# Attention, two dense blocks and SOLU on one core: x by token tile, a first chunk kept in SBUF, and stores moved to GpSimd

## The chip, the cores and the metric

The kernel runs on 1 core of one Trainium2 chip (8 cores; the others are idle). The metric is the device time of one execution in microseconds, as the median of several runs.

## The reference

`x` is (8, 8, 512, 64): 8 batches, 8 heads, 512 tokens, 64 wide. `state` is (8, 8, 32, 64). The weights come as 64-bit floats.

```python
scores = scale * x @ state.T                 # per batch and head
a = softmax(scores)                          # over the 32 states
xread = a @ state
a2 = softmax(scale * state @ x.T)            # over the 512 tokens
sread = a2 @ x
x = concat([xread, sread], tokens)           # 8 * (512 + 32) rows of 512
x = relu(x @ moe_w_in) ** 2 @ moe_w_out      # 512 -> 2048 -> 512
h = x @ moe2_w_in                            # 512 -> 1024
solu = h * softmax(h)
out = (layernorm(solu) * g_ln) @ moe2_w_out  # 1024 -> 512
```

## The kernel before

Products are made of float32 parts: each operand is split into a high and a low part, and `triple` adds three products (high by high, high by low, low by high) in one PSUM bank. The 64-bit weights are fetched as integer words, and `convert_parts` makes the two parts with six VectorE and two ScalarE operations, spread over the calls of `advance`.

Instead of `xread @ moe_w_in` the kernel forms state times weights first: `sw_part(u, j)` multiplies a block of states by unit u of w1_in (u = 4c + hp: chunk c of 512 columns, head pair hp). j = 0 serves batches 0 and 1, j = 1 batches 2 and 3. The products are evicted by ScalarE to `ev_sw` (L317), stored to DRAM in `sw_d` (L319, L321), and loaded back in another layout by `load_sw(b, c)` (L387), which gives one staging tile for each batch and chunk; `split_sw` makes the two parts. `hidden` (L134 to L136, tile `ps_h`) multiplies the softmax of a batch by them, and `project` (tile `acc`) adds the result of one f (128 of the 2048 hidden columns) times w1_out.

`attention(b)` is a list of 15 pieces. For batches 0 and 1: `trans_x` transposes one head pair of x (L125), splits it with an extra product (`split_bank`), `scores_t` makes scores, `rows_a` and `rows_b` the softmax of tokens (the last operation of `rows_b` is L491), `trans_a` transposes it for `hidden`, `cols_a`, `cols_b` and `cols_t` make the softmax of states, and `sread` multiplies it with x (L525). All these share two PSUM banks. `state_step(a_st, t)` transposes the states of batches 2t and 2t + 1 (tile `ps_st`) and splits them; `a_st` is filled from DRAM by `load_state_rows` (L273).

The opening fetches w1_in units 0 to 3 (`fetch_pair`, L647), x of batch 0 on ScalarE's queue (L424), the state rows; then runs the pieces of `attention(0)` between conversions of units 0 to 3 and `sw_part(u, 0)`; then `sw_part(u, 1)` and the rest of `attention(0)`. The main loop goes over 144 steps s of (batch, f), 16 f to a batch; batches 0 and 1 share the first 32 steps and alternate by chunks of four. `attention(1)` is put into steps 0 to 3 and the attention of a later batch into the 16 steps before it is needed. The table `when` gives the step at which each unit of w1_out ("o") and w1_in ("i") begins its conversion; fetches go out two steps earlier, and `sw_part` runs two steps later. Partial sums of a batch that is left go to `x2p_d` (L630). A converted w1_in part is also stored in `w1i_d` (L233) for later use.

Each engine takes its instructions in a fixed order that the build chose, mostly that of the program. All DMAs are issued by SyncE's queue (SP), except x of batch 0, and a DMA that waits for its data holds everything behind it on its queue. Staging tiles (`stg`), eviction tiles (`ev`) and the converted w1_in tiles have 4, 2 and 4 buffers.

Of the kernel before, what the change touches and what calls it, by code (L numbers as in the profile page):

```python
# [20 lines left out]
def memory_attention_relu2_solu(  # L21
# [15 lines left out]
    nc = tc.nc  # L37
# [48 lines left out]
    xsp = pool("xsp", 4, sa, side="right")  # L86
# [9 lines left out]
    mhalf = const.tile([P, 1], F32, name="mhalf")  # L96
    rebias = const.tile([P, 1], F32, name="rebias")
# [128 lines left out]
    def convert_w1in(u, st):  # L226

        c, k = divmod(u, NM)

        t = u_tile("w1in")  # L230

        def done():
            nc.sync.dma_start(out=w1i_d[k][:, :, c * FC : (c + 1) * FC], in_=t.bitcast(F32))  # L233
            w1u[u] = t

        flying.append(convert_parts(st, t[:, 0, :], t[:, 1, :], done))
# [28 lines left out]
    def load_state():  # L265
        a = wp.tile([P, B, NQ, 2, D], F32, tag="w", name="a_st")
        nc.vector.memset(a[:, :2], 0.0)
        nc.gpsimd.memset(a[:, 2:], 0.0)
        return a

    def load_state_rows(a, b0, b1):
        for h in range(4):
            nc.sync.dma_start(  # L273
                out=a[h * NS : (h + 1) * NS, b0:b1, :, h % 2, :],
                in_=state[b0:b1].rearrange("b (q h) n d -> h n b q d", h=4)[h],
            )

    def state_step(a, t):

        if t == 0:  # L280
            bdw[0] = wp.tile([P, 2, NQ, 4, 2 * NS, 2], F32R, tag="w", name="bdw")
            nc.vector.memset(bdw[0].bitcast(F32), 0.0)
# [18 lines left out]
    def sw_part(u, j):  # L301
# [3 lines left out]
        single = c == 0 and j < 2  # L305
        if j % 2 == 0 or single:
            sw_ev[0] = evp.tile([P, 2, 512], F32, tag="ev", name="ev_sw")
# [9 lines left out]
        nc.scalar.activation(out=ev[:, j % 2, :], in_=ps, func=AF.Copy)  # L317
        if single:
            nc.sync.dma_start(out=sw_d[hp][:, j, c * FC : (c + 1) * FC], in_=ev[:, j % 2, :])  # L319
        elif j % 2 == 1:  # L320
            nc.sync.dma_start(out=sw_d[hp][:, j - 1 : j + 1, c * FC : (c + 1) * FC], in_=ev)  # L321
# [96 lines left out]
    def load_x(b, hps=range(NHP), eng=None):  # L418
        if b == 1:
            both = wp.tile([P, NHP, NT, 2, D], F32, tag="w", name="xs_w")  # L420
        for hp in hps:
            t = both[:, hp] if b == 1 else xsp.tile([P, NT, 2, D], F32, tag="xs", name="xs")
            for i in range(2):
                (eng or nc.sync).dma_start(out=t[:, :, i], in_=x[b, 2 * hp + i].rearrange("(p t) d -> p t d", t=NT))  # L424
            xs_t.setdefault(b, []).append(t)

    def attention(b):
# [3 lines left out]
        def trans_x(hp):  # L431
            ps = bank("ps_x")
            transposes(ps, [xs_t[b][hp][:, t].rearrange("p h d -> p (h d)") for t in range(NT)])
# [83 lines left out]
        def sread(half):  # L517
# [3 lines left out]
            for hp in (2 * half, 2 * half + 1):  # L521
                for t in range(NT):
                    for i in range(2):
# [3 lines left out]
                            lhsT=xs_t[b][hp][:, t, i, :],  # L527
# [82 lines left out]
    def project(blk, f, n, gh, gl, m):  # L610
# [7 lines left out]
        if last:  # L618
# [9 lines left out]
            if m % 2 == 1:  # L628
                to = x2p_d[blk] if f + 1 < NF else x2_d[blk]
                nc.sync.dma_start(out=to[:, m - 1 : m + 1, :], in_=x2_ev[0][:, :, :n])  # L630
# [22 lines left out]
    nc.gpsimd.memset(rebias, -float(896 << 23))  # L653
    make_identity(nc, ident)
    fetch_pair(0, 0)
    load_x(0, eng=nc.scalar)
    a_st = load_state()
    load_state_rows(a_st, 0, 2)
    nc.scalar.activation(out=negi, in_=ident, func=AF.Copy, scale=-1.0)
    nc.gpsimd.memset(mhalf, -0.5)  # L660
# [6 lines left out]
    load_state_rows(a_st, 2, B)  # L667
# [12 lines left out]
    load_sw(0, 0)  # L680
# [4 lines left out]
    begin("o", 0)  # L685
    state_step(a_st, 1)
    for i in range(4):
        fetch_pair(NM + 2 * (i // 2), i % 2)
# [118 lines left out]
    when |= {("i", u): w for u, w in zip(range(AHEAD, NU), (1, 2, 3, 4, 7, 8, 9, 10, 13, 15, 16, 18))}  # L807
# [16 lines left out]
    for s, (b, f) in enumerate(items):  # L824
# [43 lines left out]
        if s == 2 * FPC - 1:  # L868
            load_sw(*chunks[2])
# [11 lines left out]
        if s // FPC + 1 < len(chunks) and chunks[s // FPC + 1][0] < B:  # L881
# [3 lines left out]
            elif s % FPC == 1:  # L885
                load_sw(*nxt)
# [101 lines left out]
```

## Time and profile before

| what | value |
|---|---|
| runs | 1136.05, 1141.4, 1140.76 us; median 1140.76 |
| profiled execution | 1139.05 us, its span 1137.3 us |
| TensorE (PE) busy | 1104.1 us, 97% |
| VectorE (DVE) busy | 706.0 us, 62% |
| ScalarE (ACT) busy | 512.7 us, 45% |
| GpSimd (POOL) busy | 43.1 us, 4% |
| mean granted clock of PE | 0.994 |

Busy shares are means over the whole span; the first 84 us differ from the rest. A granted clock of 1.00 is the upper of the two levels of PE (2.4 GHz). Lines such as L134 are those of the kernel before. "A <-B" at the end of a row of the timeline tells how long the engine had been idle and who released it.

### The profile page before, as it was taken

To read this page: it belongs to the slowest core of one execution; us is meant where nothing else is said; L and a number is where in the kernel's file an instruction comes from. 1 tells how busy PE (TensorE), PEld (TensorE's weight loads), DVE (VectorE), ACT (ScalarE), POOL (GpSimd) and SP (SyncE) were. 2 spreads that over 40 slices of the span, in tenths; PEclk is the share of its full clock that TensorE was granted. 3 is DMA by queue.
4 is the path that set the end of the run, shared out by engine and by line. 5 is a ranking of instruction groups with operands and counts; after the bars stand their busy time and mean duration, and the time that the engine had idled before them with its cause. 6 is when DMAs were issued, how large, how long until landed. Compare 5 with 4: busy or idle time off the path is not lost.

```text
span 1137.3 us, 15226 instructions
## 1 busy us (share of the span) xinstructions
PE 1104.1 (97%) x5692; PEld 911.9 (80%) x5692; DVE 706.0 (62%) x1358; ACT 512.7 (45%) x902; POOL 43.1 (4%) x59
## 2 busy tenths in 40 slices
PE   5779999999999999999999999999999999999997
PEld 3557888878888888888888889988888888888886
DVE  6389987479578488685675545664545545455442
ACT  4778987555355354342343213352433434334332
POOL 0000000001000010010000000000000000000000
PEclk9889999999999999999999999999999999999999
DMA  8688986478776652412211126420101101000010
GB/s 221 205 223 279 322 269 167 138 207 228 200 214 183 183 175 93 139 56 72 77 38 56 38 75 238 165 80 19 56 28 57 65 19 39 27 19 28 19 28 29
DMA packets 93962, 135.75 MB, mean 119 GB/s; under 512 B 45376, under 2 KB 45888, under 8 KB 93888
## 3 DMA queue, kind: packets, MB, share of 16 engines
q1 hardware_dynamic: 89664, 133.73, 37.9%
q10 hardware_dynamic: 4224, 1.05, 0.5%
q8 instruction: 45, 0.74, 0.3%
q14 instruction: 29, 0.24, 0.1%
HBM read 84.41 MB, written 50.33 MB: 118 GB/s over the span
## 4 chain that ended last, share of the span: by engine, by line
PE 88%; ACT 4%; DVE 4%; DMA 2%; issue 1%; ACTq 0%; SPq 0%; POOLq 0%; POOL 0%
PE h L738 16%; PE acc L134 10%; PE acc L136 10%; PE acc L135 10%; PE ps_h L134 6%; PE ps_o L789 5%; PE ps_h L135 5%; PE ps_h L136 5%; PE ps_o L787 5%; PE ps_o L788 5%; PE ps_t L777 2%; PE ps_sr L525 1%; PE ps_x L125 1%; PE ps_a L125 1%; DMA st<-in_moe_w_in_dram 1%
## 5 line engine op out<-in xcount | busy, mean ns | idle before, releaser
L134 PE MATMUL acc<-gh,w1out 128*128 128x512 f32 (+1 forms) x576 | 218.5, 381 | 0.5 <-ACT w1out L215 0.5
L135 PE MATMUL acc<-gl,w1out 128*128 128x512 f32 (+1 forms) x576 | 217.7, 378 | 0.1
L136 PE MATMUL acc<-gh,w1out 128*128 128x512 f32 (+1 forms) x576 | 217.3, 378 | 0.0
L738 PE MATMUL h<-w,x2h 128*128 128x512 f32 x544 | 148.6, 395 | 0.0
L584 ACT ACTIVATE r<-ps_h 128x512 f32<-128x512 f32 (+1 forms) x144 | 82.5, 573 | 132.0 <-PE ps_h L136 130.7
L586 DVE TENSOR_TENSOR r<-r,ps_h 128x512 f32<-128x512 f32 (+1 forms) x112 | 72.5, 647 | 88.6 <-ACT r L584 88.2
L134 PEld LDWEIGHTS acc<-gh,w1out 128*128 128x128 f32 x576 | 109.0, 189 | 21.9 <-ACT w1out L215 0.9
L136 PEld LDWEIGHTS acc<-gh,w1out 128*128 128x128 f32 x576 | 108.4, 188 | 20.7
L135 PEld LDWEIGHTS acc<-gl,w1out 128*128 128x128 f32 x576 | 108.4, 188 | 20.6 <-DVE gl L600 0.3
L738 PEld LDWEIGHTS h<-w,x2h 128*128 128x128 f32 x544 | 99.7, 188 | 18.8
L600 DVE TENSOR_TENSOR gl<-r,gh 128x512 fp32r<-128x512 f32 (+1 forms) x144 | 97.5, 677 | 17.7 <-ACT r L593 14.6
L134 PE MATMUL ps_h<-ah,sw 128*128 128x512 f32 x256 | 107.2, 420 | 0.9 <-ACT sw L113 0.9
L787 PE MATMUL ps_o<-w,lh 128*128 128x512 f32 x272 | 106.0, 390 | 1.0 <-ACT lh L113 1.0
L789 PE MATMUL ps_o<-w,ll 128*128 128x512 f32 x272 | 106.2, 390 | 0.6 <-DVE ll L114 0.6
L788 PE MATMUL ps_o<-w,lh 128*128 128x512 f32 x272 | 105.8, 389 | 0.0
L756 ACT ACTIVATE e<-h,nm 128x1024 f32<-128x1024 f32 x34 | 38.0, 1117 | 143.7 <-DVE nm L753 143.7
L136 PE MATMUL ps_h<-ah,sw 128*128 128x512 f32 x256 | 100.8, 396 | 0.0
L135 PE MATMUL ps_h<-al,sw 128*128 128x512 f32 x256 | 100.1, 393 | 0.0
L752 DVE TENSOR_REDUCE nm<-h 128x1 f32<-128x1024 f32 x34 | 41.6, 1225 | 83.2 <-PE h L738 83.2
L738 PE MATMUL h<-w,x2l 128*128 128x512 f32 x272 | 83.8, 389 | 0.0
L764 ACT ACTIVATE j<-e,mu 128x1024 f32<-128x1024 f32 x34 | 39.1, 1151 | 54.3 <-DVE mu L761 50.4
L114 DVE TENSOR_TENSOR sw<-stg,sw 128x512 fp32r<-128x512 f32 x64 | 44.4, 698 | 28.5 <-ACT sw L113 28.2
(162 smaller groups left out, 1734.4 us busy)
## 6 DMA issues: line engine op xcount, KB each, us to landing
stg<-sw_d SPq DMA_DIRECT2D x128, 128.0 KB, 3.3
sw_d<-ev_sw SPq DMA_DIRECT2D x28, 512.0 KB, 3.8
st<-in_moe_w_out_dram SPq DMA_DIRECT2D x24, 512.0 KB, 5.4
w1i_d<-w1in SPq DMA_DIRECT2D x16, 512.0 KB, 4.1
st<-in_moe_w_in_dram SPq DMA_DIRECT2D x16, 512.0 KB, 5.8
w1in<-w1i_d SPq DMA_DIRECT2D x32, 256.0 KB, 4.6
x_d<-ev_x SPq DMA_DIRECT2D x16, 512.0 KB, 2.7
w1in<-w1i_d SPq DMA_DIRECT2D x16, 512.0 KB, 5.3
```

The source lines that it names most:

```text
L114: nc.vector.tensor_tensor(out=lo, in0=src, in1=hi.bitcast(F32), op=ALU.subtract)
L134: nc.tensor.matmul(out=ps, lhsT=lh, rhs=rh, start=first and i == 0, stop=False)
L135: nc.tensor.matmul(out=ps, lhsT=lh, rhs=rl, start=False, stop=False)
L136: nc.tensor.matmul(out=ps, lhsT=ll, rhs=rh, start=False, stop=last and i == n - 1)
L584: nc.scalar.activation(out=r, in_=ps, func=AF.Relu)
L586: nc.vector.tensor_tensor(out=r, in0=r, in1=ps, op=ALU.mult)
L600: nc.vector.tensor_tensor(out=gl, in0=r, in1=gh.bitcast(F32), op=ALU.subtract)
L738: nc.tensor.matmul(out=ps[:, a * 512 : (a + 1) * 512], lhsT=lt[:, k, t * P : (t + 1) * P], rhs=w2[k][:, i, a * 512 : (a + 1) * 512], start ...
L752: nc.vector.tensor_reduce(out=nm, in_=ps, axis=AX.X, op=ALU.max)
L787: nc.tensor.matmul(out=ps, lhsT=a, rhs=wt[:, 0, o : o + 512], start=(k == 0), stop=False)
L788: nc.tensor.matmul(out=ps, lhsT=a, rhs=wt[:, 1, o : o + 512], start=False, stop=False)
L789: nc.tensor.matmul(out=ps, lhsT=bb, rhs=wt[:, 0, o : o + 512], start=False, stop=(k == NK - 1))
```

## The change

x of a batch is loaded in four DMAs, one for each token tile t with all 8 heads, into one tile instead of four tiles of a head pair; batch 0's loads go from ScalarE's queue to SP's, and the first state rows from SP's to ScalarE's. The pool of x tiles has one buffer. A one-column activation runs ahead of everything on ScalarE. The memset of `bdw` moves from VectorE to GpSimd.

The products of chunk 0 for j = 0 go from `ev_sw` straight to the staging tiles of batches 0 and 1 by SBUF-to-SBUF copies; `load_sw(0, 0)` and `load_sw(1, 0)` are gone. In chunk 0 two head pairs share one `ev` tile.

The fetches of w1_in units 4 to 7 stand ahead of the splitting of the first chunk; the state rows of batches 2 to 7 are loaded later, ahead of `state_step(a_st, 1)`. Units 4 to 7 begin one step earlier, and `load_sw` of the third chunk stands one step earlier. The stores of w1_in parts, of the other sw products and of partial sums are issued by GpSimd.

```diff
-    xsp = pool("xsp", 4, sa, side="right")
+    xsp = pool("xsp", 1, sa, side="right")
...
+    warm = const.tile([P, 1], F32, name="warm")
...
         def done():
-            nc.sync.dma_start(out=w1i_d[k][:, :, c * FC : (c + 1) * FC], in_=t.bitcast(F32))
+            nc.gpsimd.dma_start(out=w1i_d[k][:, :, c * FC : (c + 1) * FC], in_=t.bitcast(F32))
...
-        nc.gpsimd.memset(a[:, 2:], 0.0)
...
-            bdw[0] = wp.tile([P, 2, NQ, 4, 2 * NS, 2], F32R, tag="w", name="bdw")
-            nc.vector.memset(bdw[0].bitcast(F32), 0.0)
...
-        single = c == 0 and j < 2
-        if j % 2 == 0 or single:
+
+        single = c == 0
+        at = i if single else j
+        if at == 0:
             sw_ev[0] = evp.tile([P, 2, 512], F32, tag="ev", name="ev_sw")
...
-        nc.scalar.activation(out=ev[:, j % 2, :], in_=ps, func=AF.Copy)
-        if single:
-            nc.sync.dma_start(out=sw_d[hp][:, j, c * FC : (c + 1) * FC], in_=ev[:, j % 2, :])
-        elif j % 2 == 1:
-            nc.sync.dma_start(out=sw_d[hp][:, j - 1 : j + 1, c * FC : (c + 1) * FC], in_=ev)
+        nc.scalar.activation(out=ev[:, at, :], in_=ps, func=AF.Copy)
+        if single and j == 0:
+
+            for b in range(2):
+                if hp == 0:
+                    loading[b, 0] = stgp.tile([P, 2, 512], F32, tag="stg", name="stg")
+                nc.sync.dma_start(
+                    out=loading[b, 0][i * 2 * NS : (i + 1) * 2 * NS, hp // 2, :], in_=ev[b::2, at, :]
+                )
+        elif single:
+            nc.gpsimd.dma_start(out=sw_d[hp][:, j, c * FC : (c + 1) * FC], in_=ev[:, at, :])
+        elif j == 1:
+            nc.gpsimd.dma_start(out=sw_d[hp][:, j - 1 : j + 1, c * FC : (c + 1) * FC], in_=ev)
...
+    def load_x(b):
+        pl, tag = (wp, "w") if b == 1 else (xsp, "xs")
+        xs_t[b] = pl.tile([P, NT, H, D], F32, tag=tag, name="xs")
+        for t in range(NT):
+            nc.sync.dma_start(out=xs_t[b][:, t], in_=x[b].rearrange("h (p t) d -> t p h d", t=NT)[t])
...
-                nc.sync.dma_start(out=to[:, m - 1 : m + 1, :], in_=x2_ev[0][:, :, :n])
+                (nc.gpsimd if f + 1 < NF else nc.sync).dma_start(out=to[:, m - 1 : m + 1, :], in_=x2_ev[0][:, :, :n])
...
     nc.gpsimd.memset(rebias, -float(896 << 23))
+    nc.scalar.activation(out=warm, in_=rebias, func=AF.Copy)
     make_identity(nc, ident)
     fetch_pair(0, 0)
-    load_x(0, eng=nc.scalar)
+    load_x(0)
     a_st = load_state()
-    load_state_rows(a_st, 0, 2)
+    load_state_rows(a_st, 0, 2, nc.scalar)
+    bdw[0] = wp.tile([P, 2, NQ, 4, 2 * NS, 2], F32R, tag="w", name="bdw")
+    nc.gpsimd.memset(bdw[0].bitcast(F32), 0.0)
+    nc.gpsimd.memset(a_st[:, 2:], 0.0)
+    nc.gpsimd.memset(mhalf, -0.5)
     nc.scalar.activation(out=negi, in_=ident, func=AF.Copy, scale=-1.0)
-    nc.gpsimd.memset(mhalf, -0.5)
...
     state_step(a_st, 0)
-    load_state_rows(a_st, 2, B)
     load_x(1)
...
     sw_part(NM - 1, 0)
-    load_sw(0, 0)
+    for i in range(4):
+        fetch_pair(NM + 2 * (i // 2), i % 2)
     while len(att) > 5:
...
     begin("o", 0)
+    load_state_rows(a_st, 2, B, nc.sync)
     state_step(a_st, 1)
-    for i in range(4):
-        fetch_pair(NM + 2 * (i // 2), i % 2)
...
-    when |= {("i", u): w for u, w in zip(range(AHEAD, NU), (1, 2, 3, 4, 7, 8, 9, 10, 13, 15, 16, 18))}
+    when |= {("i", u): w for u, w in zip(range(AHEAD, NU), (0, 1, 2, 3, 7, 8, 9, 10, 13, 15, 16, 18))}
...
-        if s == 2 * FPC - 1:
+        if s == 2 * FPC - 2:
             load_sw(*chunks[2])
...
             elif s % FPC == 1:
-                load_sw(*nxt)
+                if nxt not in loading:
+                    load_sw(*nxt)
```

## Rows read from the trace of the kernel before

**Rows 1.** The page's 40 equal slices: PE's busy share, in tenths.

```profile
PE   5779999999999999999999999999999999999997
```

**Rows 2.** Stages of the span: length, each engine's busy time, granted clock, DMA.

```profile
core 0: us, PE busy (x) PEld busy (x) DVE busy (x) ACT busy (x) POOL busy (x), PEclk, DMA share, GB/s
0.00:13.00 13.00, 1.95 (x9) 1.58 (x9) 6.00 (x11) 3.77 (x7) 2.10 (x9) 1.00 0.87 226
...
28.10:33.80 5.70, 0.93 (x7) 0.72 (x8) 5.70 (x17) 3.36 (x7) 0.00 (x0) 0.89 0.80 300
33.80:38.80 5.00, 4.94 (x17) 3.20 (x17) 0.54 (x2) 3.48 (x7) 0.00 (x0) 0.50 0.00 0
38.80:48.10 9.30, 8.08 (x94) 6.35 (x94) 1.27 (x3) 5.28 (x11) 0.00 (x0) 0.97 0.55 174
48.10:65.30 17.20, 16.65 (x79) 12.20 (x77) 10.24 (x19) 15.38 (x29) 0.00 (x0) 1.00 0.89 272
65.30:72.40 7.10, 2.30 (x9) 1.63 (x10) 6.39 (x18) 4.24 (x8) 0.00 (x0) 0.84 0.96 192
72.40:84.00 11.60, 10.66 (x96) 8.69 (x95) 11.23 (x28) 8.07 (x16) 0.00 (x0) 0.81 0.77 248
84.00:180.00 96.00, 95.00 (x423) 76.55 (x423) 89.43 (x175) 82.31 (x150) 0.00 (x0) 1.00 0.85 278
```

**Rows 3.** Timeline of the first 13 us: start, duration, engine, line, operation.

```profile
0.74 7.83 ACTq L424 DMA_DIRECT2D xs<-in_x_dram  x8
1.42 3.70 SPq L273 DMA_DIRECT2D a_st<-in_state_dram  x4
8.14 1.09 PE L287 MATMUL ps_st<-ident,a_st 128*128 128x128 f32 x4 [8.14 <-DMA a_st<-in_state_dram]
8.65 1.28 ACT L203 ACT_TABLE_LOAD   x1 [8.65 <-DVE bdw L282]
9.02 1.06 PE L125 MATMUL ps_x<-ident,xs 128*128 128x128 f32 x4
12.85 0.58 ACT L118 ACTIVATE xh<-ps_x 128x512 fp32r<-128x512 f32 x1
```

**Rows 4.** Timeline of SP's queue from 39 to 49 us.

```profile
39.28 1.20 SPq L319 DMA_DIRECT2D sw_d<-ev_sw  x2
...
44.75 2.00 SPq L647 DMA_DIRECT2D st64w<-in_moe_w_in_dram  x4
...
48.49 0.64 SPq L157 DMA_DIRECT2D st<-in_moe_w_out_dram  x1
```

**Rows 5.** Timeline of PE and ACT between 26 and 48 us.

```profile
26.01 0.39 PE L136 MATMUL ps_sw<-w1in,bdw 128*128 128x512 f32 x1
37.23 1.12 PE L287 MATMUL ps_st<-ident,a_st 128*128 128x128 f32 x4
38.67 0.59 ACT L317 ACTIVATE ev_sw<-ps_sw 128x512 f32<-128x512 f32 x1
47.02 0.62 ACT L113 ACTIVATE sw<-stg 128x512 fp32r<-128x512 f32 x1
```

**Rows 6.** Timeline of DVE from 57 to 70 us, three of its operations.

```profile
57.31 0.43 DVE L202 TENSOR_SCALAR cz<-st 128x512 uint32<-128x512 uint32 x1
...
60.22 0.68 DVE L208 SCALAR_TENSOR_TENSOR cu<-st,cu 128x512 f32<-128x512 uint32 x1
...
69.64 0.68 DVE L491 TENSOR_TENSOR e<-e,sm 128x512 f32<-128x512 f32 x1
```

**Rows 7.** DMA issues of the opening: count, KB each, median us to landing.

```profile
a_st<-in_state_dram SPq DMA_DIRECT2D x4, 96.0 KB, 7.8
```

**Rows 8.** Stores of converted w1_in on SP: issue in ns, minimum, median, maximum.

```profile
L233 SPq DMA_DIRECT2D w1i_d<-w1in x16: 512/554/1155, 24.3 to 159.1; - x16
```

**Rows 9.** A later window's loads of x, their time to landing, and first transposes.

```profile
387.86 2.83 SPq L424 DMA_DIRECT2D xs<-in_x_dram  x4
396.49 0.60 PE L125 MATMUL ps_x<-ident,xs 128*128 128x128 f32 x4
DMA to landing us min/median/max: 2.5/3.3/6.5
```

More of the change, by code (lines that the diff above doesn't have):

```diff
@@ L267, in load_state, with load_state_rows @@
         nc.vector.memset(a[:, :2], 0.0)
-        nc.gpsimd.memset(a[:, 2:], 0.0)
         return a
-    def load_state_rows(a, b0, b1):
+    def load_state_rows(a, b0, b1, eng):
         for h in range(4):
-            nc.sync.dma_start(
+            eng.dma_start(
                 out=a[h * NS : (h + 1) * NS, b0:b1, :, h % 2, :],
@@ L278, in state_step @@
     def state_step(a, t):
-        if t == 0:
-            bdw[0] = wp.tile([P, 2, NQ, 4, 2 * NS, 2], F32R, tag="w", name="bdw")
-            nc.vector.memset(bdw[0].bitcast(F32), 0.0)
         ps = bank("ps_st")
@@ L416, in memory_attention_relu2_solu @@
     a1_t = {}
[L418 to L425, printed above, removed]
+    def load_x(b):
[3 more added lines that the diff above has]
+            nc.sync.dma_start(out=xs_t[b][:, t], in_=x[b].rearrange("h (p t) d -> t p h d", t=NT)[t])
     def attention(b):
@@ L432, in trans_x @@
             ps = bank("ps_x")
-            transposes(ps, [xs_t[b][hp][:, t].rearrange("p h d -> p (h d)") for t in range(NT)])
+            transposes(ps, [xs_t[b][:, t, 2 * hp : 2 * hp + 2].rearrange("p h d -> p (h d)") for t in range(NT)])
             xh = xtp.tile([P, S], F32R, tag="xh", name="xh")
@@ L526, in sread @@
                             out=ps[i * D : (i + 1) * D, hp * NS : (hp + 1) * NS],
-                            lhsT=xs_t[b][hp][:, t, i, :],
+                            lhsT=xs_t[b][:, t, h, :],
                             rhs=v["e2", t // 2][:, t % 2, h * NS : (h + 1) * NS],
```

## The prediction, made before the change was run

> **What bounds the kernel now.** I began with the page's 40 slices. TensorE (PE) is short of full in the first three slices and the last one [rows 1], so a change to the opening can only win what the opening loses. Then I cut the opening into stages and read busy time and granted clock of each [rows 2]; PE's busy time there subtracts from the length to give its idle time.
>
> - 0 to 13 us: PE idles 11.05 us. The timeline of the start [rows 3] says why: the state rows arrive at 8.14 us, the first x transposes run at 9.02, but ScalarE (ACT) has spent its queue on eight x loads until 8.57, loads its table from 8.65 to 9.93, and takes up `xh`, which is waiting since about 10.1, only at 12.85.
> - 28.1 to 33.8: 4.77 us idle: the softmax of `attention(0)`, alone.
> - 33.8 to 38.8: full, but at granted clock 0.50, which is the lower of the two levels (1.2 GHz); it had fallen after the idle stretch. The same work at the upper level would be about 2.5 us shorter.
> - 38.8 to 48.1: 1.22 us idle. The first `hidden` could not start before its chunk had gone to DRAM and back: evicted at 38.67, stores issued from 39.28, and only from 47.02 split by ACT for the products [rows 4, 5].
> - 48.1 to 65.3: 0.55 us idle; ACT is busy 15.38 of 17.20.
> - 65.3 to 72.4: 4.80 us idle, and here VectorE (DVE) is busy 6.39 of 7.10. PE stands at `trans_a` of `attention(1)`, whose last DVE operation runs at 69.64 [rows 6]. The clock falls again: 0.84 over 7.10 us and 0.81 over the next 11.60 us make 2.3 + 4.4 = 6.7 us at the lower level; PE had work in about 6.2 of them, a loss of 3.1.
> - 72.4 to 84: 0.94 us idle. 84 to 180: 1.00 us idle in 96, DVE busy 89.43.
>
> From 84 us on PE is full. So the change can win part of what lies before, and it can lose anywhere, if it slows DVE or delays a buffer.
>
> **The change, part by part.** The sum goes against the profiled execution, 1139.05 us, which is 1.7 below the median of the three runs.
>
> *Start.* ACT loses the eight x issues and gets four issues of state rows; a one-column activation asks for the table early; the 2048-element memset leaves DVE for GpSimd (Pool). ACT's part of the delay goes: after the transposes of x, `xh` can be taken at once. What now sets the start is whether data arrive. The state rows wait on ACT for the table load: at most 1.28 us later than 8.14 [rows 3], at best no later. x needs all of its 1 MB before the first transpose (the tile is cut by token, where before a head pair was enough), but the DMA engines moved 226 GB/s over 0 to 13 us [rows 2], 1.6 MB by about 9 after the first bytes at about 2. I take PE's start at 9.0; two sets of transposes took 1.94 us (8.14 to 10.08), so `xh` starts at 10.9 in place of 12.85: **-2.0** (bounds -2.8 at 8.14, -1.5 at 9.4). Pool has nothing else then, and its memsets are needed only at about 9.
>
> *State rows of batches 2 to 7*, moved on SP from ahead of x of batch 1 to behind the j = 0 copies and four weight loads. They feed `state_step(1)`, which ran at 37.23 [rows 5], with PE's in-order queue behind it: the j = 1 products, `cols_t`, `sread`, `attention(1)`. With -2.0 it could run at 35.2. The last j = 0 product ended at 26.4 [rows 5], so now at about 24.4; its copies go out by 26, four weight loads take 2.00 us [rows 4], so the first rows go out at about 28 and the last by 30; their landing took 7.8 [rows 7]. That gives 36 to 38, or 34 where the engines are free sooner: **+1.0** (0 to +3.0). This is the one place where a move adds a wait.
>
> *First chunk from SBUF to SBUF.* Four stores of 256 KB to DRAM and eight reloads become eight copies of 128 KB, and no load waits for a store any more. Two `ev` halves per tile also remove the wait of the third eviction for the first store. The chunk is ready before `trans_a` ends. PE was short by only 1.22 us there, as it had other work: **-0.8** (0 to -1.2). Chunk (1, 0) came from DRAM too; it no longer does, but the wait it caused ACT lay beside DVE's, so nothing.
>
> *Next weights at another place.* The loads of w1_in units 4 to 7 move ahead of SP's waits: from 44.75 to about 26; the load of w1_out 1, at 48.49, follows them up [rows 4]. DVE was busy 1.27 of 9.30 and 0.54 of 5.00 us before 48.1 [rows 2], and then had to convert while `attention(1)` waited: one tile is three masks of 0.43 and three operations of 0.68 us, 3.3 in all. Between the mask at 57.31 and the operation at 69.64 [rows 6] lie twelve conversion operations, one whole tile and half of two more; they are some 6.5 us, and as each starts a little before the last one ends, about 5.3 of DVE's time. With data and free DVE time earlier, and unit 4 begun a step earlier by the table of due steps, these go ahead of the chain. The chain to `trans_a` then shortens by up to 5.3, the idle 4.80 us shrink, and the clock has less reason to fall (3.1). All of it would be -7.9; I take the chain's 5.3 and a little of the clock: **-5.5** (0 to -7.9). After 84 us all must still be fed by DVE; it can, as the same operations only moved earlier.
>
> *38 stores on Pool* (16 of w1_in parts, 16 of sw products, 6 of partial sums). On SP such a store takes 0.51 to 1.16 us of issue, 0.55 in the median [rows 8], and SP stood behind stores that waited for their data, which held the loads in [rows 4]. Freed, this gain is already counted above. No Pool DMA occurs before, so its price is unknown: below, nothing (Pool is idle); above, that each holds a DVE operation for an issue, 0.55 us as on SP up to 0.98, ACT's mean for the x loads [rows 3]. I take nothing, since the consumers are steps away, and keep the rest as a rival. The Trainium skill, DMA: Bandwidth & Descriptors, "Issuing engines are not separate DMA queues", says that another issuing engine saves only the sequencer's issue time; by it the move would give about 38 x 0.55 us of SP time and nothing to PE. Here the queue's order is what counts, not the issue.
>
> *x tiles of later batches.* One tile in place of four, so all loads wait for the last `sread`. In the window shown they then start at 387.86. If four loads of twice the size issue in the 2.83 us of four before, they land 3.3 later, at 394.0, and PE wants them at 396.49 [rows 9]: 2.5 us to spare. If the issue takes twice as long, they are 0.3 late; if the landing takes the longest seen, 6.5, more. I take the first, 0.
>
> Sum: -2.0 + 1.0 - 0.8 - 5.5 = -7.3, **1131.8 us**.
>
> **Rivals.**
>
> *A: the moved waits eat it.* The chain from `attention(0)` to `attention(1)` is one line: if the state rows come at the late bound (+3.0), the start's 2.0 and the first chunk's 0.8 are spent, and the conversions give only about 2: 1137. For it: PE is in order and the rows are last in SP's queue. Against: the DMA engines moved nothing from 33.8 to 38.8 [rows 2], so there is room for them to come.
>
> *B: Pool's stores hold DVE (slower).* Some 28 of the 38 fall after 84 us, where DVE has 96 - 89.43 = 6.57 us left [rows 2]. At 0.98 each it is 27.4 - 6.6 = 20.8 lost, 1152; at 0.55, 8.8, 1140. From 0.50 a store, (7.3 + 6.6) / 28, it undoes the gain, from 0.70 the kernel is slower by over 0.5%. For it: DVE's masks of 512 elements take 0.43 beside 0.68 for two-input operations of the same size [rows 6], so they run in some faster mode of their own, which another engine's work may cost them. Against: no row here shows Pool and DVE in each other's way, and an idle Pool takes 38 issues easily. The Trainium skill, SBUF — State Buffer, "Who interferes with whom", says that a DVE operation in a two-port mode and a GpSimd operation lock each other out of a shared port pair for a whole instruction, and that stores from GpSimd wait for descriptors so long. By that the stores land later, and masks may wait; no run here shows its size.
>
> *C: the x tile is late.* If the larger loads issue in twice 2.83 us and land after 6.5, they come at 400.0, 3.5 us late [rows 9]; in five windows (batches 3 to 7) that is 17.5, 1149. It makes the kernel slower than before from 1.5 us a window. Against: 3.3 is the median, and the spare of 2.5.
>
> *D: PE's gaps close and the clock stays up.* If the early chunk also fills the 4.77 us at 28.1 to 33.8 and both low stretches (2.5, 3.1) shrink: another 8 of these 10.4 us, 1124. Against: in that gap nothing but `attention(0)` can be ready.
>
> **How the numbers follow.** Forecast 0.50, A 0.26, B 0.13, C 0.04, D 0.07. A measurement here can tell about 0.5%, 5.7 us. The forecast and D are faster by more: 0.57; A is within: 0.26; B and C slower: 0.17. The likeliest alone spans 1126 to 1135. For 8 in 10 the range reaches over A and the lower part of B, and down to D: 1122 to 1143.
>
> **What would show it.** Right: `xh` at about 11 us in place of 12.85; the first `ps_h` well before 48; w1_out 1 converted on DVE before 57; the idle stretch before `trans_a` of `attention(1)` below 3 us, the end of the opening some 8 us earlier, and the later windows as long as before. Wrong: PE waiting on `a_st` at about 35 to 39; DVE operations after 84 us longer or with idle time before them that Pool ends; PE waiting for x at the start of a window; or an order of conversions on DVE that has not moved.

## The result, and the profile after

The changed kernel takes 1147.86 us in the median (1147.20 to 1149.77, 5 runs), beside 1140.76 us (1136.05 to 1141.40, 5 runs) of the kernel before on the same chip: ratio 1.0082, 95% interval [1.0067, 1.0096]. It is slower by 0.8%, against a forecast of 1131.8 us, and outside the range of 1122 to 1143. The two medians alone differ by less, 7.1 us or 0.6%, since the kernel before scattered here; in the later runs its medians lie between 1137.64 and 1138.33, which 1147.86 exceeds by 0.8 to 0.9%. The profiled execution took 1149.77 us with a span of 1147.9 us, 10.6 more than before.

The page's 40 slices of PE, which answer to [rows 1], look no worse than before:

```profile
PE   5888989999999999999999999999999999999997
```

The stages do [rows 2]; the columns are the same.

```profile
0.00:13.00 13.00, 4.59 (x13) 2.87 (x13) 5.71 (x12) 5.49 (x11) 4.65 (x11) 1.00 0.97 237
28.10:33.80 5.70, 1.28 (x5) 0.94 (x6) 5.70 (x17) 4.85 (x10) 0.00 (x0) 0.79 0.97 350
33.80:38.80 5.00, 4.74 (x14) 3.54 (x14) 1.53 (x4) 2.78 (x5) 0.00 (x0) 0.56 0.84 166
38.80:48.10 9.30, 7.93 (x36) 5.82 (x36) 4.91 (x11) 8.37 (x16) 0.74 (x1) 1.00 0.50 191
48.10:65.30 17.20, 16.98 (x137) 13.15 (x136) 16.74 (x36) 14.23 (x28) 3.95 (x6) 1.00 0.89 275
65.30:72.40 7.10, 4.26 (x22) 3.08 (x21) 6.45 (x17) 4.35 (x8) 0.10 (x1) 1.00 0.18 74
72.40:84.00 11.60, 11.12 (x74) 8.45 (x75) 8.94 (x22) 9.34 (x19) 1.45 (x2) 0.71 0.33 98
84.00:180.00 96.00, 87.91 (x410) 69.70 (x407) 76.02 (x149) 72.47 (x133) 15.83 (x23) 0.98 0.75 256
```

Up to 84 us PE is busy 4.35 us more than before. From 84 to 180 it idles 8.09 in place of 1.00, and DVE is busy only 76.02 in place of 89.43, so DVE has time to spare: 9.5 us of its work had been done before 84 us already (62.40 us busy in place of 52.91), and in 84 to 180 it waits, mostly for ACT. The later windows keep their length (the first `sread` product of batch 7 stands 6.3 us later than before, that of batch 2 stood 6.1 later), and some 4 us more are lost behind 820 us.

The start answers to [rows 3] (start, duration, engine, line, operation): the table is loaded at once, and `xh` is taken at 10.73 in place of 12.85.

```profile
0.74 1.28 ACT L658 ACT_TABLE_LOAD   x1 [0.74 <-PEq L980]
8.37 1.09 PE L284 MATMUL ps_st<-ident,a_st 128*128 128x128 f32 x4 [8.37 <-DMA a_st<-in_state_dram]
10.73 0.59 ACT L119 ACTIVATE xh<-ps_x 128x512 fp32r<-128x512 f32 x1
```

Between 20 and 33 us SP's queue holds the copies of the first chunk, the next weights, which go out 18.5 us earlier than in [rows 4], and then the state rows:

```profile
20.00 6.23 SPq L322 DMA_DIRECT2D stg<-ev_sw  x7
26.27 2.10 SPq L651 DMA_DIRECT2D st64w<-in_moe_w_in_dram  x4
28.47 4.12 SPq L273 DMA_DIRECT2D a_st<-in_state_dram  x4
```

PE in the same stretch answers to [rows 5]. The first `hidden` product runs at 35.55 (before: 48.10), and all four hidden tiles of it stand ahead of `state_step(1)`, which runs at 42.51 (before: 37.23) without waiting for its rows. `attention(1)` begins at 52.33 (before: 44.57).

```profile
35.55 0.63 PE L135 MATMUL ps_h<-ah,sw 128*128 128x512 f32 x1
...
42.51 0.60 PE L284 MATMUL ps_st<-ident,a_st 128*128 128x128 f32 x4
...
52.33 0.66 PE L126 MATMUL ps_x<-ident,xs 128*128 128x128 f32 x4
```

DVE [rows 6]: the last two operations before `trans_a` of `attention(1)` run from 72.06 to 73.34; before, the last one ended at 70.32, 3.0 us earlier. Their chain on DVE, from the first maximum on, is shorter than before, 6.0 us (67.31 to 73.34) in place of 8.9 (61.42 to 70.32, the first line below is of the kernel before), but it begins 5.9 us later, when PE delivers `ps_r`. Masks and two-input operations take as long as before (0.41 to 0.43, and 0.68).

```profile
61.42 0.68 DVE L476 TENSOR_REDUCE mx<-ps_r 128x16 f32<-128x512 f32 x1
```

```profile
57.20 0.41 DVE L203 TENSOR_SCALAR cz<-st 128x512 uint32<-128x512 uint32 x1
...
58.20 0.68 DVE L209 SCALAR_TENSOR_TENSOR cu<-st,cu 128x512 f32<-128x512 uint32 x1
...
67.31 1.29 DVE L480 TENSOR_REDUCE mx<-ps_r 128x16 f32<-128x512 f32 x2 [0.65 <-PE ps_r L470]
...
72.06 1.28 DVE L495 TENSOR_TENSOR e<-e,sm 128x512 f32<-128x512 f32 x2
```

The late state rows land in 7.8 us, as before [rows 7]. The issue of a w1_in store now takes 0.69 us on Pool in the median, 0.55 on SP before [rows 8]. The loads of x [rows 9] begin at 394.41, 6.6 us later than the last four before; 6.3 of that is the shift of the whole window. They land 3.7 to 4.8 us after their issue, the first transposes run at 402.62 (before: 396.49), and PE doesn't wait for them.

```profile
a_st<-in_state_dram SPq DMA_DIRECT2D x4, 96.0 KB, 7.8
...
L234 POOL DMA_DIRECT2D w1i_d<-w1in x16: 667/687/1235, 8.8 to 152.6; - x16
...
394.41 3.22 SPq L429 DMA_DIRECT2D xs<-in_x_dram  x4
```

From the views of waits (who waited, for whom, us in total, times, longest) of SP and ACT in 0 to 200 us and of PE in 84 to 180 us: SP stands before reloads whose stores, from Pool, have not landed. The first line is the kernel before, with 2.8 us in 2 waits.

```profile
SPq L387 <- DMA sw_d<-ev_sw: 2.8, 2, 1.8
```

```profile
SPq L394 <- DMA sw_d<-ev_sw: 31.9, 9, 11.3
...
ACT sw L114 <- DMA stg<-sw_d: 6.9, 6, 2.1
ACT ev_x L629 <- DMA sw_d<-ev_sw: 4.8, 2, 3.5
...
PE acc L135 <- ACT ev_x L629: 4.0, 3, 1.5
PE ps_sw L135 <- DVE xl L115: 2.0, 1, 2.0
PE ps_x L126 <- ACT ev_sw L316: 1.2, 1, 1.2
```

Stores to `sw_d` of 256 KB landed in 5.2 us in the median (3.9 before), those of 512 KB in 4.9 (4.3), w1_in parts in 4.6 (4.1). The 256 KB stores aren't the same set: before they are eight, now four. With the same four on SP (c1 below) they land in 2.0 us, so the step to Pool's 5.2 is larger than these numbers say.

Groups of instructions of 820 to 1080 us, by form, show the tail: the products of `up` (with moe2_w_in, tile `h`) take 400 and 395 ns. Before they took 395 and 389 (the first two lines), while those of `down` (with moe2_w_out, tile `ps_o`) stay at 389.

```profile
L738 PE MATMUL h<-w,x2h 128*128 128x512 f32 x352 | 96.2, 395 | 0.0
...
L738 PE MATMUL h<-w,x2l 128*128 128x512 f32 x176 | 54.2, 389 | 0.0
```

```profile
L745 PE MATMUL h<-w,x2h 128*128 128x512 f32 x349 | 97.5, 400 | 0.0
L794 PE MATMUL ps_o<-w,lh 128*128 128x512 f32 x176 | 68.5, 389 | 0.0
...
L745 PE MATMUL h<-w,x2l 128*128 128x512 f32 x176 | 55.3, 395 | 0.0
```

The one thing the change does to that stage is a new 4-byte constant tile, `warm`: in the built program it moves every later pool on the left of SBUF by 32 bytes (`wp` from 17632 to 17664), while the x2 tiles, on the right, stay at 196576.

### The profile page after: what moved, and what is told of

Same layout as the page of the kernel before. It is cut to its first block, busy times and chain, and to the rows that moved or that the text cites. A ratio compares the mean times of both kernels' runs of the same rounds, so it can differ in the third digit from the quotient of the medians.

```text
span 1147.9 us, 15200 instructions
## 1 busy us (share of the span) xinstructions
PE 1112.3 (97%) x5692; PEld 912.5 (79%) x5692; DVE 703.3 (61%) x1357; ACT 513.6 (45%) x903; POOL 70.4 (6%) x98
## 4 chain that ended last, share of the span: by engine, by line
PE 84%; DVE 2%; DMA 1%; ACT 1%; issue 1%; POOLq 0%; POOL 0%; ACTq 0%; SPq 0%
PE h L745 16%; PE acc L136 10%; PE acc L135 10%; PE acc L137 9%; PE ps_h L135 5%; PE ps_o L796 5%; PE ps_o L794 5%; PE ps_o L795 5%; PE ps_h L136 5%; PE ps_h L137 5%; PE ps_t L784 2%; PE ps_sr L529 1%; PE ps_x L126 1%; DMA sw_d<-ev_sw 1%; PE ps_sw L379 1%; PE ps_sw L380 1%
## 5 line engine op out<-in xcount | busy, mean ns | idle before, releaser
L745 PE MATMUL h<-w,x2h 128*128 128x512 f32 x544 | 151.7, 400 | 0.0
L771 ACT ACTIVATE j<-e,mu 128x1024 f32<-128x1024 f32 x34 | 39.1, 1151 | 54.3 <-DVE mu L768 50.4
L745 PEld LDWEIGHTS h<-w,x2l 128*128 128x128 f32 x272 | 51.0, 188 | 12.4
```

Of the source, the lines that this page charges most:

```text
L745: nc.tensor.matmul(out=ps[:, a * 512 : (a + 1) * 512], lhsT=lt[:, k, t * P : (t + 1) * P], rhs=w2[k][:, i, a * 512 : (a + 1) * 512], start ...
L771: nc.scalar.activation(out=j, in_=e, func=AF.Square, bias=mu, accum_out=var)
```

## The experiments

Each run was measured beside the kernel before; ratios are to that kernel on the same chip. Where two runs are compared, an interval of the difference is worked out from those of the two ratios. Lines begin with + or - as against the kernel named.

### Stores and the shift, one at a time

**e1_sp_stores**: the changed kernel, all 38 stores on SP again.

```
-            nc.gpsimd.dma_start(out=w1i_d[k][:, :, ...], in_=t.bitcast(F32))
+            nc.sync.dma_start(out=w1i_d[k][:, :, ...], in_=t.bitcast(F32))
...
```

> The changed kernel with its 38 stores issued by SP again, all else kept. Theory 'late stores' (the stores that GpSimd issues land late, so eviction tiles come free late, PE waits 4.0 us for them after 84 us and the clock dips at 160 us): that idle time of 8 us in 84 to 180 shrinks to 1 to 2 us, and the median falls from 1147.9 by 5 to 7, to about 1142. Rival 'order' (the early first chunk let the build put four hidden products ahead of the rest of attention(0), so attention(1) starts 8 us later, and who issues the stores matters little): the idle time after 84 us stays above 5 us and the median stays at 1145 to 1149.

Measured: 1140.59 us, 1.0020 [1.0008, 1.0032], some 7 us off. PE in 84 to 180 us is nearly full again (same columns as the stages):

```profile
84.00:180.00 96.00, 94.18 (x425) 76.45 (x424) 83.14 (x158) 76.67 (x141) 0.00 (x0) 1.00 0.84 275
```

**e2_no_shift**: the changed kernel without the tile. But for the target of that one activation, its built program has the same instructions in the same order on every engine.

```
-    warm = const.tile([P, 1], F32, name="warm")
...
-    nc.scalar.activation(out=warm, in_=rebias, func=AF.Copy)
+    nc.scalar.activation(out=gcol[:, :1], in_=rebias, func=AF.Copy)
```

> The changed kernel, with the early activation writing into a column of gcol, which is loaded later, so that no tile of one column is added; every later tile of the left side then lies 32 bytes lower, as before the change. Theory 'address' (the 32 bytes make the 816 matmuls of the second block's first product slower, 400 and 395 ns in place of 395 and 389, as their moving tiles moved against the stationary ones that lie on the other side): those means return to 395 and 389, and the median falls by 4 to 5 us, to about 1143.5. Rival 'chance of that execution': no change of the median, within 1 us.

Measured: 1142.88 us, 1.0044 [1.0029, 1.0059]. The products of `up` are back at the pace of before:

```profile
L744 PE MATMUL h<-w,x2h 128*128 128x512 f32 x356 | 97.4, 395 | 0.0
...
L744 PE MATMUL h<-w,x2l 128*128 128x512 f32 x178 | 54.8, 389 | 0.0
```

**e3_before_shift**: the kernel before with an unused tile of that size; here too every engine keeps its order, with one memset more on Pool.

```
+    warm = const.tile([P, 1], F32, name="warm")
...
+    nc.gpsimd.memset(warm, 0.0)
```

> The kernel before with one unused tile of one column added, which moves every later tile of the left side up by 32 bytes; no other instruction than its memset. Theory 'address': the 816 matmuls go to 400 and 395 ns, and the median rises by 4 to 5 us, to about 1145. Rival 'chance of that execution': 1140.8, as before, within 1 us.

Measured: 1143.14 us beside 1137.86, 1.0049 [1.0032, 1.0067]. An unused tile of four bytes costs 5 us, and in the same groups:

```profile
L740 PE MATMUL h<-w,x2h 128*128 128x512 f32 x348 | 97.1, 400 | 0.0
...
L740 PE MATMUL h<-w,x2l 128*128 128x512 f32 x174 | 54.6, 395 | 0.0
```

**e4_before_pool**: the kernel before with the 38 stores on Pool, nothing else.

```
-            nc.sync.dma_start(out=w1i_d[k][:, :, ...], in_=t.bitcast(F32))
+            nc.gpsimd.dma_start(out=w1i_d[k][:, :, ...], in_=t.bitcast(F32))
...
```

> The kernel before with only the same 40-odd stores issued by GpSimd. Theory 'late stores': idle time of PE after 84 us rises from 1.0 by some us and the median rises by 2 to 6, to 1143 to 1147. Rival 'order' (GpSimd's stores alone are harmless): 1140.8 within 1.5, or faster, as SP's queue no longer stands behind them.

Measured: 1150.56 us, 1.0119 [1.0093, 1.0145], the slowest of all; PE idles 8.7 us in 84 to 180.

```profile
84.00:180.00 96.00, 87.28 (x374) 69.80 (x373) 80.36 (x159) 71.38 (x132) 15.83 (x24) 0.96 0.77 262
```

**c1_rest**: the changed kernel without the tile and with all stores on SP; both edits are those of e1 and e2.

> The changed kernel without the 32-byte shift and with all stores on SP: what is left is x by token tile, the early table, the first chunk within SBUF and the new places of loads. If the two costs add (5.0 for the shift, 7.3 for the stores), 1147.9 - 12.3 = 1135.6, or 2 us under the kernel before. Rival 'they overlap': above 1138.

Measured: 1135.73 us, 0.9979 [0.9969, 0.9989]. The two add up: the stores cost 7.1 (against e2), the shift 5, and what is left of the change is worth only 0.2%.

### Why the stores cost

**c2_w1in_only**: c1 with the 16 w1_in stores on Pool (the first pair of lines of e4).

> As the one before, but with the 16 stores of w1_in parts issued by GpSimd; nobody reads these for 32 steps. Theory 'reloads wait' (what costs is that the reloads of sw_d on SP stand at the head of SP's queue until GpSimd's store has landed, 31.9 us of waits in nine cases in the changed kernel against 2.8 in two before, and hold the fetches behind them): within 1.5 us of the kernel with all stores on SP. Rival 'GpSimd's descriptors hold VectorE': 16 of 38 stores cost about 3 of the 7.3 us.

Measured: 1139.77 us, 1.0009 [0.9999, 1.0018]: +4.0 by the medians, +0.30% (3.4 us, give or take 1.6) by the ratios, from stores whose readers come some 200 us later or more. So the late landing of `sw_d` stores can't be all.

**c9_sw_x2_pool**: c1 with the other 22 stores on Pool.

> As the 1135.7 kernel, with the 22 stores of state-times-weights tiles and of the output sums on GpSimd and the 16 w1_in stores on SP: the complement of the run that moved the 16 alone (+4.0 of the +7.1 of all 38). If the losses of the stores add up: 1138.3 to 1139.6. If it is the readers that wait for a later landing, these are the stores that are read soon, and they carry most: 1140.5 to 1143. If it is the number of transfers on GpSimd's queue in the first 150 us, 22 against 16: 1140 to 1142 too, but with landings as late as with all 38. If it is only the order of SP's queue: below 1138.

Measured: 1139.63 us, 1.0016 [1.0007, 1.0026]: +3.9 (+0.37%). The two parts give 7.9 where all 38 gave 7.1, or 0.67% where they gave 0.65%; neither kind carries the loss alone.

**c3_reload_pool**: e2 with the reloads of `sw_d` issued by Pool too, so that they can't stand in SP's queue.

```
-                    nc.sync.dma_start(
+                    (nc.gpsimd if b < 2 else nc.sync).dma_start(
                         out=st[i * 2 * NS : (i + 1) * 2 * NS, q, :],
```

> The changed kernel without the shift (1142.9), with the reloads of sw_d for batches 0 and 1 issued by GpSimd as well, behind its stores, so that SP never waits for them. Theory 'reloads wait': SP's fetches come in time, most of the cost of the stores goes: 1136 to 1139. Rival 'late landing' (stores from GpSimd land 0.6 to 1.4 us later and the chain store, reload, split is what PE waits for): 1142 to 1145, as the reloads get later too.

Measured: 1141.49 us, 1.0028 [1.0016, 1.0040], only 1.4 better than e2, which is within what can be told (0.16%, give or take 0.19%). SP no longer waits for these stores, but the reloads themselves come later: ACT waits for them 9.5 us in 84 to 180, 6.6 in e2. So the blocked SP queue is at most a small part of the loss; that 24 more transfers on Pool have a price of their own is not excluded.

**c4_three_ev**: e2 with three buffers for evictions.

```
-    evp = pool("evp", 2)
+    evp = pool("evp", 3)
```

> The changed kernel without the shift (1142.9), with three eviction tiles in place of two. Theory 'ev tiles' (PE's 4.0 us for ev_x and 1.2 us for ev_sw come from tiles that late stores hold): 1137 to 1139. Rival 'reloads wait': these waits are a part only, 1140 to 1142.

Measured: 1143.97 us, 1.0050 [1.0031, 1.0069]: no gain. ACT's wait for an eviction tile that a store still held, 4.7 us in 84 to 180 in e2, is gone, but its wait for reloads went from 6.6 to 11.9. So the buffers that the stores hold longer are not what sets the time; with them free, the wait moves to the reloads.

**c8_w1in_act**: c1 with the 16 w1_in stores on ACT.

```
-            nc.sync.dma_start(out=w1i_d[k][:, :, ...], in_=t.bitcast(F32))
+            nc.scalar.dma_start(out=w1i_d[k][:, :, ...], in_=t.bitcast(F32))
```

> As the 1135.7 kernel, with the 16 w1_in stores issued by ScalarE instead of SP (issued by GpSimd they cost 4.0: 1139.8). If the loss is that SP's queue, without these stores, reaches its waiting reloads in another order and holds what is behind them, it shows here too: 1138.5 to 1141, and SP's waits for the state-times-weights stores are near 10 us in 0 to 200 us again. If the loss lies in GpSimd's own issue and its software queue (later landings), it is gone: 1135 to 1137.5, with landings of w1_in stores at 4.7 or below; ScalarE's own 16 issues of some 0.6 us lie in stretches where it is 0.8 busy and may cost 0 to 1.5 of that.

Measured: 1138.03 us, 1.0007 [0.9998, 1.0017]: +2.3 by the medians, between the two expectations. By the ratios c8 stands 0.28% above c1 and c2 0.30%, each give or take 0.14%: the two can't be told apart. So these stores cost on ScalarE's queue as well, where each issue takes 0.52 us of ACT's time, and a part that is Pool's own is not shown. What is waited for differs: SP's reloads waited 0.7 us for `sw_d` stores here, 10.2 in c2, 2.0 in c1; ACT waited for reloads in 84 to 180 0.3, 9.3 and 2.6 us. In 84 to 180 us PE's busy time is, in c1, c2 and c8 in turn:

```profile
84.00:180.00 96.00, 94.00 (x468) 76.50 (x465) 83.06 (x159) 76.60 (x142) 0.00 (x0) 1.00 0.85 276
```

```profile
84.00:180.00 96.00, 90.44 (x417) 72.69 (x415) 79.07 (x154) 74.72 (x137) 5.50 (x8) 0.98 0.78 260
```

```profile
84.00:180.00 96.00, 93.01 (x450) 75.69 (x447) 85.19 (x164) 77.20 (x143) 0.00 (x0) 0.98 0.79 269
```

### Where the forecast gain of the rest went

**c5_rest_dram_chunk**: c1 with the first chunk through DRAM.

```
-        at = i if single else j
+        at = i if single and j == 1 else j % 2
...
-                nc.sync.dma_start(
-                    out=loading[b, 0][i * 2 * NS : (i + 1) * 2 * NS, hp // 2, :], in_=ev[b::2, at, :]
+            nc.sync.dma_start(out=sw_d[hp][:, j, c * FC : (c + 1) * FC], in_=ev[:, at, :])
...
+    load_sw(0, 0)
```

> As the changed kernel with the 32-byte shift undone and all stores on SP (measured 1135.7), and with the first chunk going through DRAM again. Theory (the early chunk makes the build's order put the first hidden products ahead of attention(1), which then starts 7.8 us later and whose x tile, scores and sums finish 2.3 us later): hidden comes back to about 48 us, ps_x of attention(1) to 42 to 45 us, and the time is 1131 to 1134. Rival (the start of attention(1) sets nothing, the chunk's shorter way is a gain of its own): 1136.5 to 1138, and the later windows begin later than at 1135.7's kernel by as much.

Measured: 1137.18 us, 0.9992 [0.9982, 1.0003], 1.5 us above c1, which is within what can be told. My theory fell: `attention(1)` began at 55.2 us, later still, so it isn't the early chunk that puts it late.

**c10_start_only**: the kernel before with the start of the change and nothing else.

```
+    nc.scalar.activation(out=gcol[:, :1], in_=rebias, func=AF.Copy)
...
-    load_x(0, eng=nc.scalar)
+    load_x(0)
...
-    load_state_rows(a_st, 0, 2)
+    load_state_rows(a_st, 0, 2, nc.scalar)
+    bdw[0] = wp.tile([P, 2, NQ, 4, 2 * NS, 2], F32R, tag="w", name="bdw")
+    nc.gpsimd.memset(bdw[0].bitcast(F32), 0.0)
...
```

> The kernel before with the start of the change alone (x by token tile on SP, state rows 0 and 1 on ScalarE, the table loaded early, the block-diagonal tile cleared by GpSimd), with no new constant tile. If the 2.1 us by which the first x tile is split earlier are kept to the end: 1136.0 to 1136.6 beside 1138.3 of the kernel before, that is as much as the whole rest of the change gave (2.2 to 2.6), and the moves of the next weights and of the first chunk together gave nothing. If the start is eaten in the gap before the state step or by the weights' loads behind x: 1137.8 to 1139, and the gain of the rest is the weights' moves.

Measured: 1136.09 us beside 1138.19, 0.9980 [0.9969, 0.9991]. The start alone gives as much as c1, which holds the other moves too.

**d2_start_rows**: c10 with the state rows of batches 2 to 7 loaded late.

```
-    load_state_rows(a_st, 2, B, nc.sync)
...
     begin("o", 0)
+    load_state_rows(a_st, 2, B, nc.sync)
```

> The kernel before with the start of the change (1136.1) and with the state rows of batches 2 to 7 loaded later, as in the change; nothing else moved. Theory: the first hidden products go ahead of the second state step, attention(1) begins at 52 us or later in place of 41, and the time is 1138 to 1141. Rival (the order of these products is of no account, the rows land in time): 1135.5 to 1136.8.

Measured: 1140.05 us, 1.0020 [1.0010, 1.0030], +4. The order turns round as expected, and PE idles 14.6 us between 28.1 and 180 us where it idled 10.1 in c10. PE's first transposes of x of `attention(1)` in c10, in d2, and in d4 below:

```profile
41.12 0.66 PE L125 MATMUL ps_x<-ident,xs 128*128 128x128 f32 x4
```

```profile
54.91 0.66 PE L125 MATMUL ps_x<-ident,xs 128*128 128x128 f32 x4
```

```profile
42.40 0.66 PE L125 MATMUL ps_x<-ident,xs 128*128 128x128 f32 x4
```

**d3_start_chunk**: c10 with the chunk from SBUF to SBUF.

> The kernel before with the start of the change (1136.1) and with the first chunk of state times weights from SBUF to SBUF; rows and weights as before. Between the two kernels with the late rows the chunk was worth 1.45: if it is worth as much here, 1134.2 to 1135.2; if it only mattered because the hidden products came first there, 1135.7 to 1136.8, since here attention(1) comes first and hides the chunk's way.

Measured: 1138.00 us, 0.9999 [0.9989, 1.0009]: alone the chunk gains nothing, it costs 1.9 (0.19%, give or take 0.15%).

**d4_rest_rows_early**: c1 with the state rows where the kernel before loads them (d2's lines the other way round).

> The whole change with the 32-byte shift undone, all stores on SP (1135.7 so far) and the state rows of batches 2 to 7 loaded where the kernel before loads them. Theory: attention(1) begins at 41 to 45 us again, and the time is 1131 to 1133.5, the 2 to 4 us that the late rows cost. Rival (the late rows cost nothing): 1135.2 to 1136.2.

Measured: 1137.97 us, 1.0000 [0.9991, 1.0010]. The order came back (42.40), the gain didn't: beside the early chunk the late rows gain 2.2 (0.21%, give or take 0.14%).

**d1_start_weights**: c10 with loads and conversions of the next weights at the change's places, and with the reload of `chunks[2]` (the second chunk of batch 0, "the second reload" below) a step earlier as in the change.

```
+    for i in range(4):
+        fetch_pair(NM + 2 * (i // 2), i % 2)
...
-    when |= {... (1, 2, 3, 4, 7, 8, 9, 10, 13, 15, 16, 18))}
+    when |= {... (0, 1, 2, 3, 7, 8, 9, 10, 13, 15, 16, 18))}
...
-        if s == 2 * FPC - 1:
+        if s == 2 * FPC - 2:
             load_sw(*chunks[2])
```

> The kernel before with the start of the change (1136.1) and with the next weights' loads and conversions moved as in the change, the state rows of batches 2 to 7 and the first chunk left as before. New theory (it is the later rows of the state that make the build set the first four hidden products ahead of the second state step, and attention(1) late; the weights' move is a gain for itself, as forecast, though smaller): attention(1) begins at 41 to 44 us and the time is 1132 to 1135. Rival (the weights' move itself costs the 1.1 us that it and the rows cost together): 1136.8 to 1138.

Measured: 1137.00 us, 0.9989 [0.9980, 0.9999], +0.9. That is within what can be told from nothing (0.09%, give or take 0.15%), and not the gain of 1 to 4 us of the theory.

**f2_start_when**: c10 with the table `when` of d1 alone.

> The kernel before with the start of the change (1136.1) and with the conversions of the next w1_in tiles one step earlier, nothing else (the earlier place of their loads alone leaves every engine's order of instructions as it was). Theory (with attention(1) beginning at 41 to 43 us, the earlier conversions come ahead of its softmax sums on VectorE, where they came behind them at 1136.1): the second sum of exponentials ends at 66 us or later (62.1 at 1136.1), PE is idle 5 us or more between 48 and 84 (4.0), and the time is 1136.8 to 1138. Rival (the step at which the second chunk is read back, which was moved as well, made the 0.9): 1135.6 to 1136.5.

Measured: 1136.49 us, 0.9985 [0.9975, 0.9995]. The sums and PE's idle time (5.2 us) came as the theory said, but of the time only 0.4, within what can be told. DVE's operations of `attention(1)`'s softmax in c10, then in f2: in f2 two tiles' conversions stand between the maxima and the sums, in c10 part of one tile's.

```profile
55.59 1.29 DVE L469 TENSOR_REDUCE mx<-ps_r 128x16 f32<-128x512 f32 x2
...
59.52 0.68 DVE L481 TENSOR_REDUCE sm<-e 128x16 f32<-128x512 f32 x1
...
61.39 0.68 DVE L481 TENSOR_REDUCE sm<-e 128x16 f32<-128x512 f32 x1
```

```profile
56.48 1.29 DVE L469 TENSOR_REDUCE mx<-ps_r 128x16 f32<-128x512 f32 x2
...
65.35 1.27 DVE L481 TENSOR_REDUCE sm<-e 128x16 f32<-128x512 f32 x2
```

**c7_rest_old_steps**: c1 with `when` and the second reload at the steps of the kernel before.

> The whole change with the 32-byte shift undone and all stores on SP (1135.7), the conversions and the second chunk's reading back at the steps of the kernel before. Theory (with the late rows attention(1) begins at 54 us, and the earlier conversions are through before its softmax; at the old steps they come into it): 1137 to 1140, and PE is idle 5 us or more between 48 and 84 (3.3 at 1135.7). Rival (the steps are of no account): 1135.2 to 1136.3.

Measured: 1133.13 us beside 1137.64, 0.9959 [0.9946, 0.9971]: the fastest of all, and against my theory. The earlier conversions cost here too, 0.20%, give or take 0.16%. In the traces `attention(1)` begins at 51.9 in place of c1's 54.3, and its maxima follow (c7, then c1):

```profile
66.37 1.29 DVE L479 TENSOR_REDUCE mx<-ps_r 128x16 f32<-128x512 f32 x2
```

```profile
69.24 1.29 DVE L479 TENSOR_REDUCE mx<-ps_r 128x16 f32<-128x512 f32 x2 [0.65 <-PE ps_r L469]
```

But 1.8 us of both differences were there by 28.1 us, where PE's order is the same in c1 and c7. In c1's profiled execution the products of 512 columns took 0.63 to 0.79 us each until 19.5 us, in c7's only until 13, and 0.39 to 0.51 after that. So the same 56 instructions of PE were busy longer (c7, then c1), though the granted clock reads 1.00 in both:

```profile
0.00:28.10 28.10, 14.46 (x56) 9.10 (x56) 19.14 (x40) 16.69 (x31) 3.85 (x10) 1.00 1.07 286
```

```profile
0.00:28.10 28.10, 16.99 (x56) 10.69 (x56) 17.43 (x37) 16.07 (x29) 3.84 (x10) 1.00 1.05 281
```

The changed kernel and e2, whose instructions stand in the same order, differ just so (16.34 and 14.15, and 14.28 in e1, which has the tile), so it goes with the execution and not with the edit. Beyond that, PE idles 1.7 us more in 84 to 180 in c1 (2.00) than in c7 (0.30).

## Why the prediction was wrong

By differences of ratios, c10, c7, c1, e2 and the changed kernel in a line:

| part | forecast, us | measured |
|---|---|---|
| start | -2.0 | -0.20% (-2.3 us) |
| late rows, chunk, loads (c7 against c10) | +1.0 -0.8, loads in the next line | -0.21% (-2.4 us) |
| conversions and second reload a step earlier (c1 against c7) | with the loads -5.5 | +0.20% (+2.3 us) |
| 38 stores on Pool (e2 against c1) | 0 | +0.65% (+7.4 us) |
| the tile `warm` | none | +0.38% (+4.3 us) |
| sum | -7.3 | +0.82% (+9.3 us) |

Each ratio has an interval of 0.1 to 0.15% to either side, so each line after the first can be off by some 2 us. Five of the six signs that I had named for being right came: `xh` at 10.73, the first `ps_h` at 35.55, w1_out 1 converted on DVE from 45.4, the idle stretch down to 2.84 us, the later windows as long as before. Only the end of the opening didn't come earlier. Those five are signs of single parts, and none of them looks at 84 to 180 us, where the time was lost.

*Start*: right in mechanism and size (`xh` at 10.73, forecast 10.9; c10 keeps 2.1 to 2.3 us of it to the end).

*38 stores on Pool, "I take nothing, since the consumers are steps away"*: this step failed most: a term put at nothing measured 7.4 us. The consumers of the w1_in stores are far away, and those 16 still cost 3 to 4. Rival B named the right edit, but its mechanism isn't what the trace shows: masks still take 0.42 us, and DVE has time to spare; only the later landings came, as it said. By the Trainium skill, DMA: Bandwidth & Descriptors, "Issuing engines are not separate DMA queues", another issuing engine saves only issue time; the measurement shows a loss that this rule doesn't contain, and it decides. What makes the loss stays open in the main: not the eviction buffers (c4), little of it SP blocked by reloads (c3), and of the w1_in part no share is shown to be Pool's alone (c8). With each such move the build also sets the instructions of the engines in another order: in the built programs some 160 of VectorE's 1323 stand at another place in c2 than in c1, and some 360 in c8. No run here separates that from the later landings.

*The tile*: the sum had no term for it, since a 4-byte tile that one activation writes seemed free. e2 and e3 show its price from both sides, with every engine's order unchanged, and the 816 products of `up`, each 5 to 6 ns longer, account for 4.4 us of it.

*Next weights, -5.5*: this step failed in the sign too. No run shows a gain (d1, f2), and c1 against c7 shows a loss of 2.3. Their loads did come early, the first conversions ran on DVE at 45.4, before the chain, as forecast, and the chain shortened by 2.9 us. But it then began 5.9 us later, since `attention(1)` began 7.8 later on PE: I had taken the chain's start as given. And I took "earlier" to mean "ahead of the chain" for all conversions. Units 5 to 7 moved a step earlier too, and where `attention(1)` begins early (f2) they came from behind the softmax sums to a place ahead of them. The 4.80 us gap did shrink to 2.84, but the work that fills it is PE's own from other stretches. Why c1 idles more than c7 behind 84 us stays open. The earlier place of the loads alone changes no engine's order of instructions on top of c10, so it was not run by itself.

*State rows, +1.0, and first chunk, -0.8*: I priced them as waits. There was no wait; PE never stood at `a_st` after the start. What moved was the order: with late rows the build puts four hidden tiles ahead of `state_step(1)`. With the chunk through DRAM they then wait (d2: first product at 37.25 us, +4.0); with the chunk in SBUF they fill the softmax gap (c7: 33.37 us). The chunk alone costs 1.9, the rows alone 4.0, both together, with the loads, gain 2.4. They are one edit, and my sum treated them as two. PE's idle time between 28.1 and 180 us goes along: 10.1 us in c10, 14.6 in d2, 8.2 in c7. So the reversed order is seen to cost or gain with the chunk's way; it isn't tested by itself. Why d3 alone loses 1.9 stays open: it idles 10.1 as c10 does, but its granted clock in 48.1 to 84 is 0.90 beside 0.95, and from 66 to 70 us it is 0.52 with PE full. These 3.6 us more at the lower level (0.05 x 35.9 x 2) could be worth up to 1.8, an estimate from one execution of each.

*x tiles of later batches, 0*: right. Rivals A, C and D did not occur.

## What to carry to other kernels

Before a store is moved to an idle engine's queue because its reader is far away, try a few of them alone: here 16 stores whose readers come 200 us later cost about as much as 22 that are read soon. When a move changes what is ready first, expect the instruction order to change, and try edits that feed each other together and apart (2 x 2), since their prices don't add. After any added tile, however small, compare the mean times of the same products in stages the change doesn't touch. The version to keep is c7: the change without its constant tile, with its stores on SP and its conversions at the old steps, 0.4% faster than the kernel before.

## What the runs showed of the hardware

A shift of the pools on the left by 32 bytes slowed the products of `up`, whose two operands lie on different sides of SBUF, from 395 to 400 and from 389 to 395 ns; those of `down`, whose operands both moved, kept 389. It was so in the three kernels with the shift (the changed one, e1, e3) and in none without it (the kernel before, e2, e4, c1); which relation of addresses does it was not tried. The w1_in stores, of 512 KB, took 0.69 us to issue from Pool, 0.55 from SP. The same four stores of 256 KB landed in 5.5 us from Pool (e2) and 2.0 from SP (c1), the twelve `sw_d` stores of 512 KB in 5.1 and 3.5. In the first 28.1 us the same 56 instructions of PE were busy 14.0 us in one profiled execution (c10) and 17.0 in another (c1), with a granted clock of 1.00 in both rows, so places in two traces can differ by some 2 us with no edit behind it.
